# Moving a spectrum's halves across partitions by transfers on the SyncE queue instead of ScalarE copies, one item ahead

## The chip, the core and the metric

The kernel runs on one core of a Trainium2 chip. The core's engines are TensorE (matmuls, PE in the profile, with its weight loads as PEld), VectorE (DVE), ScalarE (ACT), GpSimd (POOL) and SyncE (SP), which here only issues transfers. Each engine works through its own instructions in a fixed order, written when the program is built, and waits at the head of that order for semaphores. SBUF has 128 partitions; matmul results land in the banks of PSUM. The metric is the device time of one execution in microseconds (us), the median of several runs.

## What is computed

The reference runs four layers in turn on a sequence of 2048 positions with 576 channels: a Fourier mixing layer, a gated long convolution, and both again.

```python
x = x + A(layernorm(x))      # real part of a 2-D DFT: Cr @ (n @ Wr) - Ci @ (n @ Wi)
x = x + B(layernorm(x))      # q * (irfft(rfft(kv) * rfft(ssm_k)) + kv * ssm_D), q = layernorm(x)
x = x + A(layernorm(x))
x = x + B(layernorm(x))
```

Here `kv` is a short convolution of `k` times `v`, the same in both B layers and independent of `x`. So the long convolution of `kv` with `ssm_k` has to be done once, and it can run beside the first A layer.

## The kernel before

**The main work.** In the first A layer (`layer`) TensorE multiplies the normalized rows with the sequence DFT matrix `c_mat`. A c-step (`tb`, `g`, `k`) loads one 128x512 block of it on SP's queue, splits it into a rounded high part (ScalarE, L91) and a remainder (VectorE, L92), and does 12 products of 512 columns into the four banks `s` and two into the bank `rm`. After 16 steps the banks are evacuated as `u`. After two groups of 16 the hidden-dimension products of the block before (`hidden`, L267, 27 products of 288 columns a piece) come in pieces between the c-steps. There are 4 blocks, and each gives 8 pieces; 24 of the pieces lie in the stretch of the change, three blocks' worth.

**The branch beside it.** The convolution is a generator, `branch` (L338), whose pieces are issued between the c-steps. It is a long DFT done as 128 points by 16 by 128 points. Its first stage writes its results to DRAM (`t_d`). The **16-point stage** reads them back as 64 items: for each of two halves `hf` of the channels, 32 groups `qg` of frequencies. An item has 128 partitions, and its columns hold the signal (288) and the kernel `ssm_k` (288). After the 16-point DFT, partitions 0 to 63 (`lo`) hold the real parts of a spectrum and 64 to 127 (`hi`) the imaginary ones. The last stage (`i2_products`) follows, in part between the last items.

For each item the stage does this:

- `load_feed` loads the item on SP's queue (tile `land`, two buffers), and `split_feed` splits it into rounded part (ScalarE) and remainder (VectorE, L492). Both run two items or more ahead.
- `mid_kernel` multiplies the kernel's columns with the 16-point DFT (three products of 288 columns into a bank of PSUM) and brings the spectrum into SBUF as `kk`, in four ScalarE instructions. `kk` has two halves of 288 columns and two buffers. The complex product needs the imaginary part beside the real one, in the partitions of the other, so three of the four copy 64 partitions from one half of the partitions to the other.
- `mid_signal` does the same DFT for the signal, and then four VectorE instructions, L505 to L508, make the complex product: `p1` overwrites `kk[:, 0, :]`, `p2` is a tile of its own.
- `mid_round` splits the product of the item before (ScalarE, then VectorE at L492), and `mid_inverse` does the inverse 16-point DFT of an item two further back, evacuates it (ScalarE) and stores it from ScalarE's queue.

The three banks `bk` serve all of these and the pieces of `hidden`.

**What sets the order.** `act` (L483) chains all ScalarE instructions of this stage in the order in which they are written. Loads with `load_after` stay behind the last `c_mat` load issued on SP's queue. Everything else is placed by a scheduler that simulates the engines at build time and issues on each engine what is ready, by the order in which it was written. The numbers that `branch` yields are shares of a budget: the main loop resumes it as its own steps pass, 3.1 for an item (0.4 + 1.6 + 1.1) and `I2_COST` = 2.0 for a piece of the last stage, 64 x 3.1 + 32 x 2.0 in all.

Of the kernel before, what the change touches and what calls it, by code (L numbers as in the profile page):

```python
# [12 lines left out]
AF = mybir.ActivationFunctionType  # L13
OP = mybir.AluOpType
# [7 lines left out]
HD = D // 2  # L22
# [22 lines left out]
I2_COST = 2.0  # L45
# [19 lines left out]
def fnet_h3_kernel(ctx: ExitStack, tc: tile.TileContext, x, c_mat, w_re, w_im, k_pad, v, shift_k,  # L65
                   ssm_k, ssm_d, f1c, i2c, midc, out):
    nc = tc.nc
# [56 lines left out]
    def lay(t, at, *sizes):  # L124

        for name, words, n in sizes:
            ring.setdefault(name, Ring()).tiles.extend(t[:, at + i * words:at + (i + 1) * words] for i in range(n))
            at += n * words
        assert at <= t.shape[1], (at, t.shape, sizes)
        return at  # L130

    def fresh(*names):
        for name in names:
            ring[name] = Ring()

    def two(v):
        return v.rearrange("p (a n) -> p a n", a=2)
# [200 lines left out]
    def branch():  # L338
# [133 lines left out]
        lo, hi = slice(0, 64), slice(64, 128)  # L472

        def mid_half(df, o):
            ps = bank()
            mm(ps[:, :HD], mc[:, 0, :], df[0][:, o:o + HD], True, False)
            mm(ps[:, :HD], mc[:, 0, :], df[1][:, o:o + HD], False, False)
            mm(ps[:, :HD], mc[:, 1, :], df[0][:, o:o + HD], False, True)
            return ps
# [3 lines left out]
        def act(*args, **kw):  # L483
            if last_act:
                with tc.issue_after(last_act[-1]):
                    last_act.append(nc.scalar.activation(*args, **kw).ins)  # L486
            else:
                last_act.append(nc.scalar.activation(*args, **kw).ins)
# [4 lines left out]

        def mid_kernel(df):
            pk, kk = mid_half(df, HD), two(ring["kk"]())
            act(kk[:, 0, :], pk[:, :HD], AF.Copy)
            act(kk[lo, 1, :], kk[hi, 0, :], AF.Copy)
            act(kk[hi, 1, :], kk[hi, 0, :], AF.Copy, scale=-1.0)
            act(kk[hi, 0, :], kk[lo, 0, :], AF.Copy)
            return kk  # L500

        def mid_signal(df, kk):
            px = mid_half(df, 0)
            p1, p2 = kk[:, 0, :], ring["p2"]()
            nc.vector.tensor_tensor(p1, px[:, :HD], p1, OP.mult)  # L505
            nc.vector.tensor_tensor(p2[lo], px[hi, :HD], kk[hi, 1, :], OP.mult)
            nc.vector.tensor_tensor(p2[hi], px[lo, :HD], kk[lo, 1, :], OP.mult)
            nc.vector.tensor_tensor(p1, p1, p2, OP.add)  # L508
            return p1

        def mid_round(p1):
            yf = two(ring["yf"]())
            act_split(yf[:, 0, :], yf[:, 1, :], p1)
            return yf

        def mid_inverse(hf, qg, yf):
            pv = bank()
            mm(pv[:, :HD], mc[:, 2, :], yf[:, 0, :], True, False)
            mm(pv[:, :HD], mc[:, 2, :], yf[:, 1, :], False, False)
            mm(pv[:, :HD], mc[:, 3, :], yf[:, 0, :], False, True)  # L520
            vo = ring["vo"]()
            act(vo, pv[:, :HD], AF.Copy)
            nc.scalar.dma_start(v_d[hf][4 * qg:4 * qg + 4].rearrange("q j c d -> (q j c) d"), vo)

        def i2_products(hf, j, fc, vf):
            yo = ring["vo"]()
            ps = bank()
            for c in range(2):
                cs = slice(c * HD, (c + 1) * HD)
                mm(ps[:, :HD], fc[:, c, :], vf[0][:, cs], c == 0, False)  # L530
                mm(ps[:, :HD], fc[:, c, :], vf[1][:, cs], False, False)
                mm(ps[:, :HD], fc[:, 2 + c, :], vf[0][:, cs], False, c == 1)
            act(yo, ps[:, :HD], AF.Copy)
            nc.scalar.dma_start(yb_d[j][:, hf * HD:(hf + 1) * HD], yo)
# [3 lines left out]
        feeds = []  # L538
# [7 lines left out]
        landed, halves, fcs, yfs = {}, {}, {}, []  # L546

        def load_feed(i):
            if i < len(feeds):
                kind, hf, q = feeds[i]  # L550
                landed[i] = ring["land"]()
                load_after(landed[i], v_d[hf][:, q].rearrange("p c d -> p (c d)") if kind else
                           t_d[hf][4 * q:4 * q + 4].rearrange("q j c s d -> (q j c) (s d)"))

        def load_fc(k):
            if k < len(rows):
                fcs[k] = quads(ring["fc"]())
                load_fr(fcs[k], i2c[rows[k]])

        def split_feed(i):  # L560
            if i < len(feeds):
                halves[i] = parts("df")
                act_split(*halves[i], landed.pop(i))
# [4 lines left out]
        for i in range(2):  # L568
            split_feed(i)
            load_feed(i + 2)  # L570
            load_fc(i)
        used, ahead, product = 0, 2, None
        for i, (kind, hf, q) in enumerate(feeds):
            df = halves.pop(i)
            if kind:
                i2_products(hf, q, fcs.pop(used), df)
                load_fc(used + ahead)
                used += 1
            else:
                if len(yfs) == MID_LAG:  # L580
                    mid_inverse(*yfs.pop(0))
                    yield 0.4
                kk = mid_kernel(df)
                if product is not None:
                    yfs.append((*product[:2], mid_round(product[2])))
                yield 1.6
                product = hf, q, mid_signal(df, kk)
            split_feed(i + 2)
            load_feed(i + ahead + 2)
            if i == last_mid:  # L590
                yield 0.4
                mid_inverse(*yfs.pop(0))
                yfs.append((*product[:2], mid_round(product[2])))
                while yfs:
                    yield 0.4
                    mid_inverse(*yfs.pop(0))
                for name, t, at, words in (("fc", m1, spare, 4 * P), ("land", flts, kk_at, D)):
                    old = ring[name]
                    held = [old.tiles[(old.n + m) % 2] for m in range(2)]
                    fresh(name)  # L600
                    lay(t, at, (name, words, 2))
                    ring[name].tiles.extend(held)
                for m in range(2):
                    load_fc(used + ahead + m)
                    load_feed(i + ahead + 3 + m)
                ahead = 4
            yield I2_COST if kind else 1.1

    def sums(src, junk):
        m = ring["stat"]()  # L610
# [96 lines left out]
    pending = []  # L707
    lay(flts, SC_AT, ("craw", NT, CRAW))
    br = branch()
    wl = load_w()  # L710
    load_x(0)
# [10 lines left out]
    used = 4  # L722
# [382 lines left out]
```

## Time and profile before

| | |
|---|---|
| median of 3 runs | 1205.37 us (1202.85 to 1206.05) |
| the profiled execution's span | 1202.1 us; its own time is not given apart from the three runs, whose fastest is 0.7 above the span |
| PE busy | 1181.4 us, 98% |
| VectorE busy | 840.0 us, 70% |
| ScalarE busy | 666.5 us, 55% |
| transfers | 261.95 MB, 218 GB/s over the span |
| 16-point stage | from about 214 to 550 us; the rest of the branch to about 616 |

The granted clock of TensorE has a mean of 0.997. How to read the rows: a group has its line, engine, operation, the tile written and the tiles read, the shape, and a count; then busy us and the mean ns of one instruction, then the idle time before them and what ended it. In a row in order of time, start and duration come first, and a bracket tells how long the engine was idle and who released it. The tile `flts` holds many small buffers, `kk`, `land`, `p2` and the raw `c_mat` blocks among them; `mid` holds the split items, `mats` the main operands. Since the ScalarE instructions of the stage come out of one helper, they all carry line L486, and are told apart by tile and shape: `flts<-bk` is an evacuation, `flts<-flts 64x288` a copy between partitions, `mid<-flts 128x288` the rounding of a product, `mid<-flts 128x576` the split of an item. A matmul's duration includes its way through the array; the distance between two starts is what it occupies.

### The profile page before, as it was taken

What the parts mean: (1) busy time and instruction counts of PE and PEld (TensorE: products, weight loads), DVE (VectorE), ACT (ScalarE), POOL (GpSimd) and SP (SyncE); (2) the same over time, 40 slices, a digit from 0 to 9 for tenths busy, and PEclk for the clock granted to TensorE, in tenths of its full rate; (3) what the DMA queues carried; (4) which work ended last, traced back from release to release, by engine and by line L of the source; (5) the groups of instructions that cost most, each with busy time, mean ns of one, the idle gap of its engine ahead of it and who ended that gap; (6) DMA issues with size and microseconds to landing.
All of it is one profiled execution on the core that took longest, in us unless ns stands there. A gap on an engine that the chain in (4) does not pass through costs nothing.

```text
span 1202.1 us, 18251 instructions
## 1 busy us (share of the span) xinstructions
PE 1181.4 (98%) x6320; PEld 1026.7 (85%) x6320; DVE 840.0 (70%) x1498; ACT 666.5 (55%) x1335; POOL 74.1 (6%) x116
## 2 busy tenths in 40 slices
PE   7999999999999999999999999999999999999997
PEld 5888888988888888888988898888888888789997
DVE  7899983678777677675347766775776777774764
ACT  6965665669877768675435666544444445450210
POOL 2200000000000000001101121000000000001111
PEclk9999999999999999999999999999999999999999
DMA  9879898546656666648967686872682686794621
GB/s 337 288 235 306 289 295 260 180 139 178 216 178 200 211 180 202 189 147 244 307 204 237 221 257 211 272 266 72 215 283 71 205 286 220 265 352 143 219 95 40
DMA packets 146110, 261.95 MB, mean 218 GB/s; under 512 B 15841, under 2 KB 44769, under 8 KB 146018
## 3 DMA queue, kind: packets, MB, share of 16 engines
q1 hardware_dynamic: 102674, 205.58, 53.2%
q10 hardware_dynamic: 36432, 42.63, 10.2%
q0 software_dynamic: 6912, 12.59, 3.9%
q8 instruction: 49, 0.80, 0.3%
q14 instruction: 43, 0.35, 0.1%
HBM read 194.09 MB, written 66.65 MB: 217 GB/s over the span
## 4 chain that ended last, share of the span: by engine, by line
PE 89%; DMA 3%; DVE 3%; ACT 3%; issue 1%; SPq 0%; POOLq 0%; ACTq 0%; POOL 0%; DVEq 0%
PE s L74 51%; PE bk L74 33%; PE rm L74 5%; DMA flts<-in_c_mat 1%; ACT flts L486 1%; DMA t<-ud 1%; ACT mid L486 0%; DMA t<-flts 0%; DVE mid L492 0%; DMA flts<-vd 0%; DMA flts<-in_ssm_k 0%; ACT u L91 0%; ACT mats L91 0%; DVE flts L172 0%; DVE mats L92 0%
## 5 line engine op out<-in xcount | busy, mean ns | idle before, releaser
L74 PE MATMUL s<-mats 128*128 128x512 f32 x2088 | 530.4, 392 | 0.4 <-DVE u L92 0.2
L74 PEld LDWEIGHTS s<-mats 128*128 128x128 f32 x2088 | 381.3, 188 | 70.6 <-DVE u L92 0.9
L92 DVE TENSOR_TENSOR mats<-flts,mats 128x512 fp32r<-128x512 f32 x206 | 141.1, 688 | 60.0 <-ACT mats L91 56.8
L91 ACT ACTIVATE mats<-flts 128x512 fp32r<-128x512 f32 x206 | 128.7, 627 | 86.4 <-PE bk L74 31.9
L74 PE MATMUL bk<-mid 128*128 128x288 f32 x768 | 131.2, 300 | 2.5 <-ACT flts L486 1.5
L74 PEld LDWEIGHTS bk<-mid 128*128 128x128 f32 x768 | 114.3, 188 | 22.1 <-ACT flts L486 9.0
L492 DVE TENSOR_TENSOR mid<-flts,mid 128x576 fp32r<-128x576 f32 (+1 forms) x160 | 101.9, 637 | 33.8 <-ACT mid L486 29.5
L74 PE MATMUL bk<-w,u 128*128 128x288 f32 x864 | 120.8, 295 | 0.1
L74 PEld LDWEIGHTS bk<-w,u 128*128 128x128 f32 x864 | 117.3, 188 | 3.6 <-ACT flts L486 1.2
L486 ACT ACTIVATE flts<-bk 128x288 f32<-128x288 f32 x160 | 61.9, 404 | 86.2 <-PE bk L74 69.8
L74 PE MATMUL rm<-mats 128*128 128x512 f32 x304 | 94.8, 390 | 0.0
L486 ACT ACTIVATE mid<-flts 128x576 fp32r<-128x576 f32 (+1 forms) x159 | 87.0, 582 | 7.5 <-DMA flts<-t 3.0
L486 ACT ACTIVATE flts<-flts 64x288 f32<-64x288 f32 x192 | 85.0, 443 | 5.9 <-ACT flts L486 0.4
L432 ACT ACTIVATE flts<-bk 128x288 f32<-128x288 f32 x128 | 49.4, 409 | 46.6 <-PE bk L74 40.1
L74 PE MATMUL bk<-f1r 128*128 128x288 f32 x384 | 66.0, 305 | 8.7 <-ACT f1r L91 6.8
L74 PEld LDWEIGHTS bk<-f1r 128*128 128x128 f32 x384 | 60.3, 194 | 16.0 <-ACT f1r L91 7.3
L74 PE MATMUL bk<-mats 128*128 128x288 f32 (+1 forms) x376 | 67.8, 317 | 0.0
L74 PEld LDWEIGHTS rm<-mats 128*128 128x128 f32 x304 | 56.9, 188 | 12.0 <-DVE flts L264 0.3
L278 DVE TENSOR_TENSOR flts<-flts,bk 128x288 f32<-128x288 f32 x48 | 21.7, 453 | 63.2 <-PE bk L74 63.2
L74 PE MATMUL s<-t,mats 128*128 128x512 f32 x264 | 65.5, 389 | 0.4 <-DVE t L92 0.4
L175 POOL TENSOR_TENSOR flts<-flts 128x1 f32<-128x1 f32 x35 | 28.5, 816 | 524.9 <-DVE flts L174 524.9
L74 PE MATMUL bk<-mats,t 128*128 128x288 f32 (+1 forms) x368 | 59.3, 303 | 0.0
(143 smaller groups left out, 1490.3 us busy)
## 6 DMA issues: line engine op xcount, KB each, us to landing
flts<-in_c_mat SPq DMA_DIRECT2D x148, 256.0 KB, 3.6
ph<-in_c_mat SPq DMA_DIRECT2D x54, 512.0 KB, 4.2
t<-flts ACTq DMA_DIRECT2D x64, 288.0 KB, 4.6
flts<-t SPq DMA_DIRECT2D x64, 288.0 KB, 2.9
flts<-in_c_mat SPq DMA_DIRECT2D x30, 512.0 KB, 4.9
vd<-flts ACTq DMA_DIRECT2D x64, 144.0 KB, 2.3
flts<-vd SPq DMA_DIRECT2D x32, 288.0 KB, 4.8
mid<-in_i2c POOLq DMA_DIRECT2D x32, 256.0 KB, 5.1
```

The lines of the kernel that those rows point to most:

```text
L74: nc.tensor.matmul(ps, lhsT, rhs, start=first, stop=last, skip_group_check=more)
L91: a = nc.scalar.activation(h, src, AF.Copy).ins
L92: return a, nc.vector.tensor_tensor(l, src, h.bitcast(F32), OP.subtract).ins
L175: pows.append(nc.gpsimd.tensor_tensor(rs, ve, mhalf, OP.pow).ins)
L278: added[:] = [nc.vector.tensor_tensor(r[:, cs], r[:, cs], ps[:, :HD], OP.add).ins]
L432: stored[:] = [nc.scalar.activation(so[:, c, :], ps[:, :HD], AF.Copy).ins]
L486: last_act.append(nc.scalar.activation(*args, **kw).ins)
L492: nc.vector.tensor_tensor(l, src, h.bitcast(F32), OP.subtract)
```

## The change

The kernel's spectrum comes out of PSUM in two ScalarE instructions of 64 partitions each, one straight into the first half of `kk`, the other into the second. Two transfers on SP's queue, inside SBUF, fill the other two quarters. The sign that one copy used to put in now stands in the VectorE instruction that uses it. The kernel's products and these transfers are issued for item i+1 ahead of the signal's products of item i; where a piece of the last stage stands between two items, at its end. For the two buffers of `kk` to suffice, the rounding of item i-1's product now stands ahead of the kernel products of item i+1, where it stood behind those of item i.

```diff
         def mid_kernel(df):
             pk, kk = mid_half(df, HD), two(ring["kk"]())
-            act(kk[:, 0, :], pk[:, :HD], AF.Copy)
-            act(kk[lo, 1, :], kk[hi, 0, :], AF.Copy)
-            act(kk[hi, 1, :], kk[hi, 0, :], AF.Copy, scale=-1.0)
-            act(kk[hi, 0, :], kk[lo, 0, :], AF.Copy)
+            act(kk[lo, 0, :], pk[lo, :HD], AF.Copy)
+            act(kk[hi, 1, :], pk[hi, :HD], AF.Copy)
+            nc.sync.dma_start(kk[hi, 0, :], kk[lo, 0, :])
+            nc.sync.dma_start(kk[lo, 1, :], kk[hi, 1, :])
             return kk
...
-            nc.vector.tensor_tensor(p2[lo], px[hi, :HD], kk[hi, 1, :], OP.mult)
+            nc.vector.scalar_tensor_tensor(p2[lo], px[hi, :HD], -1.0, kk[hi, 1, :], op0=OP.mult, op1=OP.mult)
...
-        used, ahead, product = 0, 2, None
+        used, ahead, product, spectra = 0, 2, None, {}
+
+        def kernel_ahead(i):
+            if i < len(feeds) and not feeds[i][0]:
+                spectra[i] = mid_kernel(halves[i])
+                return True
+
+        kernel_ahead(0)
         for i, (kind, hf, q) in enumerate(feeds):
             df = halves.pop(i)
             if kind:
                 i2_products(hf, q, fcs.pop(used), df)
                 load_fc(used + ahead)
                 used += 1
+                if kernel_ahead(i + 1):
+                    yield 1.2
             else:
                 if len(yfs) == MID_LAG:
                     mid_inverse(*yfs.pop(0))
                     yield 0.4
-                kk = mid_kernel(df)
                 if product is not None:
                     yfs.append((*product[:2], mid_round(product[2])))
-                yield 1.6
-                product = hf, q, mid_signal(df, kk)
+                if kernel_ahead(i + 1):
+                    yield 1.2
+                product = hf, q, mid_signal(df, spectra.pop(i))
...
-            yield I2_COST if kind else 1.1
+            yield I2_COST if kind else 1.5
```

## The prediction

> **What bounds the kernel now.** I read the page first (busy shares), then the table of stretches, then the order of time inside the 16-point stage, and last the waits.
>
> ```profile
> span 1202.1 us, 18251 instructions
> PE 1181.4 (98%) x6320; PEld 1026.7 (85%) x6320; DVE 840.0 (70%) x1498; ACT 666.5 (55%) x1335; POOL 74.1 (6%) x116
> 300.00:340.00 40.00, 39.56 (x205) 33.79 (x204) 33.10 (x65) 34.27 (x71) 0.00 (x0) 1.00 0.64 202
> ```
>
> TensorE is busy all along. The third line is one stretch of the stage: PE 39.56 of 40 us, DVE 33.10, ACT 34.27, clock 1.00, DMA share 0.64. ScalarE is loaded, but it is not the engine without gaps. The stage's steady part, in order of time (start, duration, engine, line), shows it:
>
> ```profile
> 305.49 1.53 PE L74 MATMUL s<-mats 128*128 128x512 f32 x6
> ...
> 306.19 0.41 ACT L486 ACTIVATE flts<-bk 128x288 f32<-128x288 f32 x1 [0.49 <-DVE flts L508]
> 306.63 1.37 ACT L486 ACTIVATE flts<-flts 64x288 f32<-64x288 f32 x3
> ...
> 308.03 1.02 ACT L486 ACTIVATE mid<-flts 128x288 fp32r<-128x288 f32 x2
> 308.04 0.46 DVE L505 TENSOR_TENSOR flts<-bk,flts 128x288 f32<-128x288 f32 x1 [1.26 <-ACT flts L486]
> 308.51 0.46 DVE L492 TENSOR_TENSOR mid<-flts,mid 128x288 fp32r<-128x288 f32 x1
> ...
> 309.48 0.45 DVE L507 TENSOR_TENSOR flts<-bk,flts 64x288 f32<-64x288 f32 x1
> ...
> 309.88 1.53 PE L74 MATMUL s<-mats 128*128 128x512 f32 x6
> ...
> 310.64 0.45 DVE L508 TENSOR_TENSOR flts<-flts 128x288 f32<-128x288 f32 x1
> 310.75 0.32 SPq L159 DMA_DIRECT2D flts<-t  x1
> ...
> 311.72 0.33 SPq L159 DMA_DIRECT2D flts<-in_c_mat  x1
> ...
> 317.83 0.63 ACT L91 ACTIVATE mats<-flts 128x512 fp32r<-128x512 f32 x1
> ...
> 309.25 0.80 PE bk L74 x6
> 310.04 1.37 PE s L74 x6
> ```
>
> One c-step lasts 309.88 - 305.49 = 4.39 us and carries one item. The last two rows are from the chain that ended last: six 512-column products take 1.37 (0.228 each), six of 288 columns 0.80 (0.133 each). A step has 12 products of the `s` banks, two of the remainder and 9 of the item: 14 x 0.228 + 9 x 0.133 = 4.39. There is nothing to gain in a step of this kind, whatever ScalarE does. What can be gained are the places where TensorE waits for the item. All waits of 220 to 550 us that touch the change (total, times, longest), the last one SP's own:
>
> ```profile
> DVE flts L505 <- ACT flts L486: 36.5, 24, 2.7
> PEld bk L74 <- ACT flts L486: 10.1, 27, 1.0
> PEld bk L74 <- DVE flts L507: 3.0, 7, 0.9
> ACT mid L486 <- DMA flts<-t: 3.0, 5, 0.9
> SPq L159 <- DVE mid L492: 173.7, 73, 5.8
> ```
>
> The waits of the weight load are not all lost, since a load runs ahead of its matmul. One such place (the first four rows; the last two belong to the part on the transfers):
>
> ```profile
> 335.00 1.52 PE L74 MATMUL s<-mats 128*128 128x512 f32 x6
> ...
> 336.45 0.45 DVE L507 TENSOR_TENSOR flts<-bk,flts 64x288 f32<-64x288 f32 x1
> ...
> 336.95 0.43 PEld L74 LDWEIGHTS bk<-mid 128*128 128x128 f32 x3 [0.86 <-DVE flts L507]
> 336.95 0.66 PE L74 MATMUL bk<-mid 128*128 128x288 f32 x3 [0.44 <-DVE flts L507]
> ...
> 346.14 0.46 DVE L505 TENSOR_TENSOR flts<-bk,flts 128x288 f32<-128x288 f32 x1 [2.65 <-ACT flts L486]
> ...
> 353.15 0.46 DVE L505 TENSOR_TENSOR flts<-bk,flts 128x288 f32<-128x288 f32 x1
> ```
>
> Six products from 335.00 at 0.228 would have let the next begin at 336.37; it began at 336.95. So 0.58 of the 0.86 was lost and 0.28 was covered. Applied to all: 10.1 - 27 x 0.28 = 2.5 us lost behind ScalarE's evacuations, 3.0 - 7 x 0.28 = 1.0 behind the products' last read of their bank. Waits shorter than 0.28 lose nothing instead of a negative amount, so the true sum is somewhat above 3.5; I put 5 us as the ceiling of what this change can win.
>
> **The change part by part.** Durations by line, from 220 to 550 us (and one from 214 to 616):
>
> ```profile
> L486 ACT ACTIVATE flts<-flts 64x288 f32<-64x288 f32 x192 | 85.0, 443 | 5.9 <-ACT flts L486 0.4
> L486 ACT ACTIVATE flts<-bk 128x288 f32<-128x288 f32 x135 | 51.7, 404 | 54.8 <-PE bk L74 46.7 <-ACT flts L486 5.5 <-DVE flts L508 1.0
> L486 ACT ACTIVATE mid<-flts 128x288 fp32r<-128x288 f32 x62 | 27.6, 445 | 2.3 <-DVE flts L508 0.8
> L492 DVE TENSOR_TENSOR mid<-flts,mid 128x288 fp32r<-128x288 f32 x62 | 28.2, 456 | 11.1 <-ACT mid L486 10.7
> L506 DVE TENSOR_TENSOR flts<-bk,flts 64x288 f32<-64x288 f32 x63 | 29.0, 460 | 1.7
> L492 DVE TENSOR_TENSOR mid<-flts,mid 128x576 fp32r<-128x576 f32 x75 | 56.8, 758 | 3.7 <-ACT mid L486 1.7
> ...
> L232 DVE SCALAR_TENSOR_TENSOR w<-flts,w 128x576 fp32r<-128x576 f32 (+1 forms) x2 | 1.5, 757 | 0.1
> ```
>
> *Removed on ScalarE.* Per item one evacuation of 128x288 (404 ns) and three copies of 64x288 (443 each): 1.73 us. In their place two evacuations of 64x288. ScalarE's time goes by columns, not partitions (443 for 64x288, 445 for 128x288 out of the same tile), so each is 404: 0.81. Saved: 0.92 x 64 = 59 us of ScalarE. As PE has no gap in a steady step, what this is worth is 0 to 5 us (the ceiling). I take half, -2.5: the evacuations that came late behind three copies come earlier, but the second edit below puts something else in front of half of them.
>
> *The multiplication by -1 on VectorE.* L506 becomes a scalar_tensor_tensor. At 128x576 this form took 757 ns, the plain one 758: nothing. Bounds: 0 and a few hundredths per item, on an engine with a gap of 1.26 us ahead of L505.
>
> *The rounding of the last product goes ahead of the kernel's evacuation.* There are two `kk` buffers, and the products of item i+1 now go into the one whose product i-1 is being rounded. So in ScalarE's fixed order the first evacuation of item i+1 stands behind the rounding (445) and must wait for VectorE's subtraction, which reads the same buffer. By the rows at 308.03 and 308.51 that subtraction ended at 308.97, 0.94 after the rounding began. Before, this bank was released 0.41 after the inverse's; now 0.94 + 2 x 0.40 = 1.74: its bank is held 1.3 us longer, and behind ScalarE's wait stand the next split of a feed and whatever c split is queued there. For 64 items that is 86 us of a bank held longer. What reaches TensorE of such a delay is shown by the nearest row of the same three banks: VectorE waited 36.5 us for ScalarE with the signal's bank full, and TensorE lost 1.0 us behind it. By that share 86 us cost 2.4. Bounds: 0 (the freed 0.92 pays for it) and 13 x 0.94 = 12 (half of the 27 waits for ScalarE's evacuations are for this bank, and each grows in full). I take +2.3.
>
> *Two transfers on SP.* No transfer inside SBUF stands in this trace. Nearest are these, with us to landing:
>
> ```profile
> flts<-t SPq DMA_DIRECT2D x62, 288.0 KB, 2.9
> flts<-in_c_mat SPq DMA_DIRECT2D x53, 256.0 KB, 3.1
> vd<-flts ACTq DMA_DIRECT2D x61, 144.0 KB, 2.3
> DMA to landing us min/median/max: 2.6/2.9/6.1
> ```
>
> (the last line is for the `t` loads). The new ones hold 64 x 288 x 4 bytes, 72 KB, each, and they are issued right beside a `t` and a `c_mat` load, as the rows at 310.75 and 311.72 show. Lower bound 2.3 (the store of 144 KB), upper 6.1; I take 2.9, the loads on the same queue, plus 0.32 for the second's issue: 3.2. Is it hidden? The buffer goes round once in two items: four products of VectorE 4 x 0.455 = 1.82 and a feed's subtraction among them 0.76, rounding and subtraction 0.94, two evacuations 0.81, issue 0.32: 4.65 us, and then the transfer; with 3.2 it is 7.85. Two steady items last 8.78, so up to 4.1 us of landing are hidden. After a hidden-layer piece items come closer: from the L505 at 346.14 to the one at 353.15, two items later, are 7.0 us. Of the 62 such distances between the stage's 64 L505, 13 are shorter than 7.85, by 9 us together. That is VectorE's lateness at most; by the share above (1.0 of 36.5) 0.3 of it reach TensorE. Bounds: 0 and the 9 in full; I take +0.3. If the cover is gone, each us of landing over 4.1 costs a us per two items, 32 us in all.
>
> The Trainium skill, page "DMA: Bandwidth & Descriptors", section "Anatomy of one DMA — SWDGE (gpsimd) path", gives about 2.0 us plus bytes / 436e3 for one DMA: an estimate of 2.2 by that page, with which both transfers would be hidden everywhere and this term 0. That fit is for the other kind of queue; the rows above are slower.
>
> *SP's queue.* Two issues more per item, 0.64 us, beside 0.65 for the two loads now; SP idles for most of a step, 173.7 us of it waiting to reload a feed. A transfer's wait for ScalarE's evacuation holds up the next c load and feed load behind it. A feed's split comes after that evacuation in ScalarE's order, so its reload is ready later anyway: 0. A c load issued at 311.72 lands 3.1 later, at 314.8, and is split at 317.83 (two buffers; the split between takes the other): 3 us of slack, so 0. Where feeds are late already (3.0 us in five places) it may be a few tenths; bounds 0 and 1.5, inside the rounding of the sum.
>
> *Order of issue.* Per item the pacing still adds up to 3.1 (0.4 + 1.6 + 1.1 before, 0.4 + 1.2 + 1.5 now); only the first kernel product comes without a share, 1.2 of the stage's 262 (64 x 3.1 + 32 x 2.0): nothing. The first item waits once for a transfer (0 to 2.9 us); TensorE has c-steps to do: 0.
>
> Sum: -2.5 + 2.3 + 0.3 = +0.1 us. Against the profiled execution: 1202.1 of span to 1202.2. The median of the runs, 1205.37, lies 3.3 above that span, and I leave that as it is: 1205.5.
>
> **The rivals.**
>
> *Faster: ScalarE's relief counts in full.* For it: the copies lead directly to the longest waits of VectorE (2.65 at 346.14). The bank of the signal is emptied as soon as it is full, and the rounding finds VectorE idle. Then all of the ceiling goes: 1205.4 - 5 = 1200.4. Against it: ScalarE's new wait inside the same order.
>
> *Slower: the evacuation behind the rounding becomes TensorE's wait.* There are three banks, and a piece of the hidden layer holds one for its 27 products; with the kernel's held 1.3 us longer, one is left. Half of the 27 waits, each 0.94 longer, is +12, less the 2.5 won: 1205.4 + 9.5 = 1215 at worst, and with half of them 1209.5. I price it at 1211. It decides as soon as more than six of these waits grow in full. Against it: in a steady step the item has 4.39 us and the bank is needed again a whole item later.
>
> *Slower: the transfers land late.* If the second half waits for the first and both for the load ahead of them, landing grows from 3.2 to half as much again, 4.8; that is 0.7 over the 4.1 that two steady items hide, x 32 pairs = 22, and if only the pairs beside a late load are hit, half of it: 1205.4 + 11 = 1216. It decides from a landing of 4.1 us. For it: `t` loads reached 6.1. Against it: their median is 2.9. A rule of the Trainium skill, page "DMA: Bandwidth & Descriptors", section "Rules for kernel authors", speaks for this one: two transfers to disjoint partition halves serialize, and one should use a single transfer of 128 partitions. No transfer in this trace shows that.
>
> **How the numbers follow.** What a measurement of this kernel can tell from no change is about 0.3%, 3.6 us. No change (1205.5, from 1201.8 to 1209): 0.36. Faster in full: 0.28. Rounding ahead of the evacuation: 0.21. Late transfers: 0.15. So faster 0.28, same 0.36, slower 0.36. The range goes from 1200 (the full ceiling) to 1213.5, leaving out 0.06 below and 0.13 above; the likeliest case's own range is 1201.8 to 1209.
>
> **What would show it.** Right, if VectorE's L505 no longer waits for ScalarE, the steady step is still 4.39 us, the new transfers land in 2.3 to 3.5 us, and ScalarE's first half evacuation waits for the subtraction of the rounding, 0.3 to 0.9 us per item. TensorE's weight loads for the item should still wait some 10 to 14 us. The faster rival shows as that sum falling below 6; the second rival as it passing 20, with ScalarE's half evacuations named as the releaser; the third as VectorE's products waiting for a transfer for over 20 us in total. The prediction is wrong if the items' order on TensorE changes so much that stalls at the borders of the c blocks or at the stage's two ends grow to several us each.

## The result: slower by 0.75%

The changed kernel took 1214.17 us (1213.29 to 1214.56, 4 runs) against 1204.85 us for the kernel before, in the same comparison. The ratio is 1.0075, with a 95% interval of 1.0061 to 1.0089: 9 us. The forecast was no change, 1205.5 us, with a range up to 1213.5. The time lies just outside the range, and the likeliest case did not come.

The profiled execution has a span of 1212.6 us. The page of the changed kernel, its busy row and the one stretch shown before:

```profile
span 1212.6 us, 18555 instructions
PE 1186.9 (98%) x6320; PEld 1027.3 (85%) x6320; DVE 840.7 (69%) x1498; ACT 615.9 (51%) x1207; POOL 74.0 (6%) x116
...
300.00:340.00 40.00, 40.00 (x204) 33.88 (x203) 31.66 (x63) 26.16 (x54) 0.00 (x0) 1.00 0.77 231
```

ScalarE fell from 666.5 to 615.9 us, 51 of the 59 us that the sum said. TensorE's busy time rose by 5.5 us for the same 6320 matmuls and its share stayed at 98%; so busy shares tell nothing here, and the waits do. The waits of 220 to 560 us in the changed kernel (total, times, longest), the last two SP's own:

```profile
ACT flts L486 <- DVE mid L492: 23.4, 32, 3.8
...
ACT mid L486 <- DVE flts L508: 14.8, 18, 1.8
PEld bk L74 <- ACT mid L486: 10.5, 20, 1.1
...
PEld bk L74 <- DVE mid L492: 8.7, 18, 1.3
DVE flts L505 <- DMA flts<-flts: 6.0, 6, 2.9
...
PEld bk L74 <- ACT flts L486: 3.9, 11, 0.6
...
PEld bk L74 <- DVE flts L507: 0.2, 1, 0.2
...
SPq L498 <- ACT flts L486: 91.4, 56, 4.3
SPq L159 <- DVE mid L492: 70.6, 65, 4.0
```

The waits that the change was to remove did fall: TensorE behind ScalarE's evacuations from 10.1 to 3.9 us, behind L507 from 3.0 to 0.2. VectorE's wait for the kernel's spectrum went from 36.5 (for ScalarE) to 6.0 us (for transfers). In their place stands a wait that the kernel before hardly had (0.7 us): TensorE's weight loads for the item wait 10.5 + 8.7 us for the tile `mid`, that is, for the split of a feed, first its rounded part (ScalarE), then its remainder (VectorE). And ScalarE waits 23.4 us with its evacuations for the rounding's subtraction, in 32 of the 64 items, most often 0.58 to 0.59 us.

How the one wait leads to the other shows best among the hidden-layer pieces at the start of the stage. In order of time:

```profile
228.86 0.44 ACT L486 ACTIVATE mid<-flts 128x288 fp32r<-128x288 f32 x1 [2.42 <-issue]
229.34 0.46 DVE L492 TENSOR_TENSOR mid<-flts,mid 128x288 fp32r<-128x288 f32 x1 [0.56 <-ACT mid L486]
229.89 0.84 ACT L486 ACTIVATE flts<-bk 64x288 f32<-64x288 f32 x2 [0.58 <-DVE mid L492]
...
230.75 0.68 ACT L486 ACTIVATE mid<-flts 128x576 fp32r<-128x576 f32 x1
...
231.48 0.19 PEld L74 LDWEIGHTS bk<-mid 128*128 128x128 f32 x1 [1.09 <-ACT mid L486]
```

The last product is rounded, its subtraction follows on VectorE, only then come the two half evacuations of the kernel's spectrum (0.58 us of waiting in front of them), and behind them the split of the feed two items on. The kernel's products of that very feed are what TensorE wants next, and their first load waits 1.09 us for the split.

In the stretch without hidden-layer pieces four steps in a row became longer, from about 318 to 336 us:

```profile
319.14 0.41 ACT L486 ACTIVATE flts<-bk 128x288 f32<-128x288 f32 x1
...
319.48 0.45 ACT L486 ACTIVATE mid<-flts 128x288 fp32r<-128x288 f32 x1
319.50 1.54 PE L74 MATMUL s<-mats 128*128 128x512 f32 x6
...
319.97 0.45 DVE L492 TENSOR_TENSOR mid<-flts,mid 128x288 fp32r<-128x288 f32 x1
...
320.52 0.84 ACT L486 ACTIVATE flts<-bk 64x288 f32<-64x288 f32 x2 [0.59 <-DVE mid L492]
...
321.38 0.69 ACT L486 ACTIVATE mid<-flts 128x576 fp32r<-128x576 f32 x1
321.47 0.46 DVE L505 TENSOR_TENSOR flts<-bk,flts 128x288 f32<-128x288 f32 x1 [1.05 <-PE bk L74]
...
322.43 0.45 DVE L507 TENSOR_TENSOR flts<-bk,flts 64x288 f32<-64x288 f32 x1
...
322.92 0.76 DVE L492 TENSOR_TENSOR mid<-flts,mid 128x576 fp32r<-128x576 f32 x1
...
323.10 1.16 PE L74 MATMUL bk<-mid 128*128 128x288 f32 x6
...
323.73 0.30 PEld L74 LDWEIGHTS bk<-mid 128*128 128x128 f32 x2 [0.18 <-DVE mid L492]
...
324.10 1.54 PE L74 MATMUL s<-mats 128*128 128x512 f32 x6
```

From 319.50 to 324.10 are 4.60 us, where TensorE's own work is 4.39. The same chain runs here with the same 0.59 us of waiting, but it is not what comes last: the split's rounded part is done at 322.07, and its remainder begins at 322.92, behind L505 to L507 in VectorE's order, which had waited 1.05 us for the signal's products on TensorE. The kernel's products then wait 0.18 us for that remainder. So this step is a loop from the signal's products over VectorE to the kernel's products of the next step. It costs 0.2 us in each of the four steps, and the other steps of this stretch take about 4.4 us or less.

To compare kernels I add up, from the trace, the distances between successive starts of matmuls beyond the usual ones (0.132 us for 288 columns, 0.227 for 512), where they exceed 15 ns, between 214 and 570 us of the span: 12.6 us before, 22.4 us after. The difference of 9.8 us is the slowdown (the spans differ by 10.5, the medians by 9.3). Both traces hold 6320 matmuls, so missing records do not make the difference. By stretch, 214 to 292 us went from 4.1 to 8.2, 292 to 338 stayed at 0.8, and 338 to 570 went from 7.7 to 13.4; the kernels run shifted by some us, so these borders are rough. The stretch of the long steps thus adds nothing to the difference; the loss lies ahead of it and behind it, where other pieces stand between the items. Where the trace names what released the weight load or the matmul behind such a distance, 11.1 of the 22.4 us end with the split of a feed (5.7 its rounded part, 5.4 its remainder), and 0.3 of the 12.6 in the kernel before.

### The profile page after: what moved, and what is told of

It is laid out like the page before. It is cut to its first block, busy times and chain, and to the rows that moved or that the text cites. A ratio compares the mean times of both kernels' runs of the same rounds, so it can differ in the third digit from the quotient of the medians.

```text
span 1212.6 us, 18555 instructions
## 1 busy us (share of the span) xinstructions
PE 1186.9 (98%) x6320; PEld 1027.3 (85%) x6320; DVE 840.7 (69%) x1498; ACT 615.9 (51%) x1207; POOL 74.0 (6%) x116
## 4 chain that ended last, share of the span: by engine, by line
PE 82%; DMA 6%; DVE 5%; ACT 3%; issue 3%; SPq 0%; POOLq 0%; ACTq 0%; DVEq 0%
PE s L74 47%; PE bk L74 31%; PE rm L74 5%; DVE mid L492 2%; DMA t<-flts 1%; ACT mid L486 1%; DMA flts<-flts 1%; DMA early<-in_x 1%; ACT flts L486 1%; DMA flts<-t 1%; DVE flts L506 1%; DVE flts L507 1%; DMA t<-ud 1%; DMA mid<-in_i2c 0%; DMA flts<-in_c_mat 0%
## 5 line engine op out<-in xcount | busy, mean ns | idle before, releaser
L486 ACT ACTIVATE flts<-bk 64x288 f32<-64x288 f32 (+1 forms) x224 | 91.2, 408 | 121.7 <-PE bk L74 92.0
L74 PE MATMUL bk<-mid 128*128 128x288 f32 x768 | 137.4, 303 | 7.4 <-ACT mid L486 2.8
L486 ACT ACTIVATE mid<-flts 128x576 fp32r<-128x576 f32 (+1 forms) x159 | 92.2, 585 | 28.6 <-DVE flts L508 14.8
L432 ACT ACTIVATE flts<-bk 128x288 f32<-128x288 f32 x128 | 49.4, 409 | 46.6 <-PE bk L74 40.6
L74 PEld LDWEIGHTS s<-t,mats 128*128 128x128 f32 x264 | 49.5, 188 | 10.7 <-DVE t L92 0.5
```

The lines of the kernel that those rows point to most:

```text
L74: nc.tensor.matmul(ps, lhsT, rhs, start=first, stop=last, skip_group_check=more)
L432: stored[:] = [nc.scalar.activation(so[:, c, :], ps[:, :HD], AF.Copy).ins]
```

## The experiments

Two theories were left after the traces. **Lead**: the kernel's products now stand one item ahead, and with them the need for the feed's split; `split_feed` kept its place, so its lead shrank from two items to one. **Round**: the rounding now holds the `kk` buffer that the next evacuation wants, so ScalarE waits for VectorE in the middle of its fixed order. The rival was **transfers**: they land late or hold up SP's queue. All ratios are to the kernel before, in the same comparison, and the last column is the sum just defined (in e_short the stage runs on to about 614 us, so its sum falls short). The order on every engine is set anew when a kernel is built, so each edit also moves instructions that it does not name.

| run | what differs | us | ratio (95%) | lost by TensorE, us |
|---|---|---|---|---|
| after | the change | 1214.17 | 1.0075 (1.0061 to 1.0089) | 22.4 |
| e_copies | after, copies for transfers | 1220.79 | 1.0135 (1.0114 to 1.0156) | 29.9 |
| e_transfers | before, transfers for copies | 1221.44 | 1.0132 (1.0109 to 1.0154) | 28.6 |
| e_short | before, split one item later | 1255.81 | 1.0427 (1.0404 to 1.0451) | 55.3 |
| e_lead | after, split one item earlier | 1209.61 | 1.0040 (1.0026 to 1.0053) | 17.1 |
| e_late | control for e_lead | 1215.18 | 1.0084 (1.0070 to 1.0099) | 23.5 |
| e_sum | after, sum in another tile | 1209.18 | 1.0032 (1.0019 to 1.0044) | 17.0 |
| e_p2lead | e_sum and e_lead | 1206.80 | 1.0013 (0.9996 to 1.0029) | 15.4 |
| e_first | e_sum, evacuation ahead of rounding | 1217.83 | 1.0108 (1.0089 to 1.0127) | 25.7 |
| e_first_lead | e_first and e_lead | 1211.89 | 1.0064 (1.0046 to 1.0083) | 19.3 |
| e_poolq | after, transfers on GpSimd's queue | 1218.04 | 1.0108 (1.0092 to 1.0124) | 26.4 |
| e_p2leadpool | e_p2lead, GpSimd's queue | 1209.33 | 1.0031 (1.0019 to 1.0043) | 16.7 |

### One part of the change alone

e_copies keeps the new order and takes the transfers out:

```diff
-            act(kk[lo, 0, :], pk[lo, :HD], AF.Copy)
-            act(kk[hi, 1, :], pk[hi, :HD], AF.Copy)
-            nc.sync.dma_start(kk[hi, 0, :], kk[lo, 0, :])
-            nc.sync.dma_start(kk[lo, 1, :], kk[hi, 1, :])
+            (the four ScalarE instructions of before)
```

> The changed kernel's order of issue (kernel spectrum one item ahead, rounding in front of it) with the four ScalarE instructions of before in place of two evacuations and two transfers. If the SP transfers cost the 9 us (theory transfers): back to 1205 to 1207. If the feed's split is needed an item earlier (theory lead) or the evacuation waits behind the rounding (theory round): 1214 or more, since ScalarE carries 59 us more in the same order, and TensorE's weight loads for the item still wait 20 us and more for ScalarE and VectorE.

It took 1220.79 us, 0.6% more than the changed kernel, as theories lead and round had it. This run trades the transfers for the copies and so shows only that the trade is a gain in this order: with three copies more in front of it the split comes later, and TensorE waits 17.7 us for its rounded part instead of 10.5. That the transfers themselves cost the changed kernel little rests on VectorE's 6.0 us of waiting for them, and on e_p2lead below, which keeps them. The waits of 220 to 560 us:

```profile
PEld bk L74 <- ACT mid L486: 17.7, 25, 2.7
...
PEld bk L74 <- DVE mid L492: 8.7, 21, 1.0
```

e_transfers is the other half: `mid_kernel` and the sign as in the change, everything else as before.

> The order of before, with the two half evacuations and two SP transfers in place of the copies, so the transfers stand between the kernel's products and the signal's products of the same item. Theory transfers: 1214 or more, VectorE waiting 2 us and more per item for them. Theories lead and round: near before, 1203 to 1208, although VectorE now waits for transfers in most items, because a late product alone hardly reaches TensorE.

It took 1221.44 us, where theories lead and round expected 1203 to 1208 and theory transfers 1214 or more. In this order the transfers do cost: without the item's lead they lie open between the kernel's products and the signal's. That does not carry over to the changed kernel, where VectorE waits 6.0 us for them and not 27.9. In e_transfers it waits and holds the signal's bank:

```profile
DVE flts L505 <- DMA flts<-flts: 27.9, 23, 3.0
PEld bk L74 <- DVE flts L507: 18.3, 19, 2.1
...
PE bk L74 <- DVE flts L507: 10.9, 14, 1.6
```

With 28 us of waiting in front of L505, TensorE's loads wait 18.3 us behind L507. In the kernel before they waited 3.0 us with 36.5 us in front of L505. So the share of VectorE's lateness that reaches TensorE is no constant of this kernel, and it was the share on which two terms of the forecast rested, the rounding and the transfers. The transfers need the lead of an item, and each half of the change alone is worse than both together.

### The lead

e_short takes the kernel before and shortens the lead alone:

```diff
-        for i in range(2):
+        for i in range(1):
             split_feed(i)
             load_feed(i + 2)
...
-            split_feed(i + 2)
-            load_feed(i + ahead + 2)
+            split_feed(i + 1)
+            load_feed(i + ahead + 1)
```

> The kernel before, with one thing changed: each feed is loaded and split one item later, so that its 16-point products have the lead that the changed kernel's kernel products have. Theory lead: slower by 4 to 10 us, 1209 to 1214, and TensorE's item loads wait 10 us and more for the mid tile, which they hardly do now (about 1 us). If only the order of ScalarE's work is at fault (theory round): within 2 us of before.

It lost 52 us, five times what was expected, with the mark that was expected: the loads for the item wait 37.4 us for the split's rounded part, 55 times. Three rows of its order of time, one item apart:

```profile
301.35 0.19 PEld L74 LDWEIGHTS bk<-mid 128*128 128x128 f32 x1 [0.59 <-ACT mid L486]
...
306.57 0.19 PEld L74 LDWEIGHTS bk<-mid 128*128 128x128 f32 x1 [0.60 <-ACT mid L486]
...
311.79 0.19 PEld L74 LDWEIGHTS bk<-mid 128*128 128x128 f32 x1 [0.59 <-ACT mid L486]
```

From one item to the next are 5.22 us here instead of 4.39. That the loss is so much larger than the changed kernel's may be due to the three copies, which still stand in ScalarE's order here; this was not tested apart.

e_lead does the opposite to the changed kernel: `split_feed(i + 3)` and `load_feed(i + ahead + 3)`, three splits ahead of the loop, and `I2_FIRST` 38 for 37, because the last stage's first load would otherwise come before its data are stored.

> The changed kernel, with each feed loaded and split one item further ahead (and the last stage's pieces beginning one item later, because their loads would come too early otherwise), which gives the kernel's products the lead that they had before. Theory lead: 1204 to 1208, the item's weight loads no longer wait for the mid tile. Theory round: 1211 to 1215, waits move to ScalarE's evacuations. Theory transfers: 1214.

1209.61 us, between the two theories, with the marks of both: 0.35% of the 0.75% went. Its waits of 220 to 560 us:

```profile
ACT flts L486 <- DVE mid L492: 25.4, 34, 3.6
ACT mid L486 <- DVE flts L508: 23.3, 21, 2.8
PEld bk L74 <- ACT flts L486: 13.3, 27, 1.6
...
PEld bk L74 <- ACT mid L486: 1.3, 3, 0.5
```

TensorE's waits for the split are gone (10.5 to 1.3 us), and its waits for the evacuations are back (3.9 to 13.3), while ScalarE still waits 25.4 us for the subtraction. By the sum of lost distances, 5.4 us now end with the kernel's half evacuations, 0.6 in the changed kernel: with the split out of the way, the bank that the rounding's wait holds is a good part of what TensorE still waits for. The four longer steps are gone, as they are in e_sum:

```profile
315.62 1.53 PE L74 MATMUL s<-mats 128*128 128x512 f32 x6
...
320.01 1.53 PE L74 MATMUL s<-mats 128*128 128x512 f32 x6
...
324.40 1.53 PE L74 MATMUL s<-mats 128*128 128x512 f32 x6
```

e_late has the change of `I2_FIRST` alone.

> A control for the run with the longer lead: the changed kernel with only the last stage's pieces beginning one item later. If the longer lead itself gave back the 5 us: 1213 to 1215, as the changed kernel. If the later pieces did it: 1208 to 1211.

1215.18 us, as the changed kernel: the lead did it, not the later pieces.

### The rounding

e_sum frees the `kk` buffer earlier. The sum of the two products goes to `p2`, so the rounding reads that tile:

```diff
-        lay(flts, at, ("land", D, 2), ("kk", D, 2), ("vo", HD, 3), ("p2", HD, 1))
+        lay(flts, at, ("land", D, 2), ("kk", D, 2), ("p2", HD, 1), ("vo", HD, 3))
...
-            nc.vector.tensor_tensor(p1, p1, p2, OP.add)
-            return p1
+            nc.vector.tensor_tensor(p2, p1, p2, OP.add)
+            return p2
```

> The changed kernel with the sum of the products in the other product's tile, laid one place earlier so that no other buffer shares its words: the rounding no longer holds the kk buffer. In the run of this idea made before (with the tile where it was) about half of the loss went. Theory round as one of two causes: 1208 to 1211 again, ScalarE's evacuations waiting under 2 us for the subtraction of the rounding (23 us in the changed kernel).

An earlier form of it, e_p2, left `p2` where it was. There its last words are shared with a buffer of the block borders, so that at a border an item's product is overwritten; no work is left out. It took 1209.10 us, ratio 1.0042 (1.0025 to 1.0058).

> The changed kernel, but the sum of the two products is written to the other product's tile, so the kk buffer is free after the last of the four products and ScalarE's half evacuation no longer waits for the rounding's subtraction. Theory round: 1204 to 1208, TensorE's waits for the split feeds fall with it, since the split stands behind the evacuation in ScalarE's order. Theory lead: 1212 to 1215, ScalarE's wait for VectorE gone but TensorE's waits for the feeds stay. Theory transfers: 1214.

e_sum took 1209.18 us: again about half of the loss went. Its waits:

```profile
ACT mid L486 <- DVE flts L508: 32.0, 31, 2.5
PEld bk L74 <- DVE mid L492: 9.4, 22, 1.4
...
PEld bk L74 <- ACT mid L486: 6.0, 11, 1.4
...
PEld bk L74 <- ACT flts L486: 1.8, 5, 0.5
```

ScalarE's evacuations no longer wait for the subtraction (23.4 us before; no such row of any size is left), and TensorE's waits for the split's rounded part fall from 10.5 to 6.0. Those for the remainder stay (9.4).

e_p2lead has both edits.

> The changed kernel with both repairs: the sum of the products in the other product's tile (which is laid one place earlier, so that no other buffer shares its words), and the feeds split one item further ahead. Each alone gave back about 5 of the 9 us. If they are two separate costs: 1204 to 1206. If they are the same cost, seen twice: 1209 as with either.

1206.80 us, ratio 1.0013 (0.9996 to 1.0029): both repairs together gave back 0.62%, and what is left cannot be told from nothing. The single repairs gave 0.35% and 0.43%, so by the times the two costs nearly add up. By the lost distances they overlap: the repairs alone took away 5.3 and 5.4 us of the 22.4, both together 7.0. And the interval of e_p2lead overlaps those of the single ones. So it is not shown that they are two separate costs. The order of time above says why they need not be: the rounding's wait and the short lead are two links of one chain, from the rounding over the evacuations and the split to the kernel's products, and it can be cut at either. The lost distances by stretch, in us:

| stretch of the span | before | after | e_sum | e_lead | e_p2lead |
|---|---|---|---|---|---|
| 214 to 292 us | 4.1 | 8.2 | 6.6 | 8.6 | 8.2 |
| 292 to 338 us | 0.8 | 0.8 | 0.7 | 0.0 | 0.4 |
| 338 to 570 us | 7.7 | 13.4 | 9.7 | 8.4 | 6.8 |

With both repairs the later part of the stage loses less than before, and its start loses twice as much. What the start's loss consists of was not followed up. The waits of e_p2lead show where the expected gain went:

```profile
PEld bk L74 <- ACT flts L486: 7.4, 13, 1.7
...
PEld bk L74 <- DVE flts L507: 5.3, 8, 1.7
...
DVE flts L505 <- DMA flts<-flts: 2.7, 5, 0.9
```

TensorE waits 12.7 us for the item's banks, as against 13.1 in the kernel before. With some 50 us of work off ScalarE, and VectorE's 36.5 us of waiting gone, the banks come free no earlier in the few places where TensorE waits for them.

### The order on ScalarE, and the queue

e_first is e_sum with the kernel's products and evacuations issued ahead of the rounding again:

```diff
+                more = kernel_ahead(i + 1)
                 if product is not None:
                     yfs.append((*product[:2], mid_round(product[2])))
-                if kernel_ahead(i + 1):
+                if more:
                     yield 1.2
```

> The changed kernel with the sum of the products in the other product's tile, laid one place earlier, and the kernel's products and evacuations of the next item now issued ahead of the rounding, as before. Then the rounding no longer stands waiting for the sum in front of them on ScalarE. Theory round: the waits of ScalarE's rounding for the sum fall from 30 us to under 15, and the time to 1205 to 1208. Theory lead alone: 1209 to 1213, TensorE's waits for the mid tile stay over 10 us.

> The same as the run before it in this call (sum in the other product's tile, kernel's evacuations ahead of the rounding), with the feeds split one item further ahead as well. If lead and round are the two causes, what is left is ScalarE's relief: 1201 to 1205, TensorE's item loads waiting 10 us or less in all. If something else of the change costs (transfers, SP's queue, the order of TensorE's work): 1207 and more.

They took 1217.83 and 1211.89 us, each slower than its partner with the rounding in front (1209.18 and 1206.80). The first lies outside both ranges, the second in that for something else of the change that costs; as e_p2lead, which differs only in this order, is back within noise of before, it is this order that costs. ScalarE's waits for the sum did fall (from 32.0 to 9.1 us in e_first), but its evacuations wait more for TensorE:

```profile
ACT flts L486 <- PE bk L74: 91.2, 68, 3.6
PEld bk L74 <- ACT mid L486: 10.8, 23, 0.8
```

In e_sum that wait is 63.4 us. The evacuation now stands at the head of ScalarE's order before its products are done, with the rounding and the split behind it. That this is the whole cause was not tested; in e_first_lead, where the split is no longer urgent, the loss is 0.5% against e_p2lead all the same. So, with the buffer of its own, the rounding's new place is the better one; what it cost in the changed kernel came with the buffer that it shared.

e_poolq and e_p2leadpool issue the two transfers on GpSimd's queue, nothing else.

> The changed kernel with its two transfers issued from GpSimd's queue instead of SP's. If SP's queue, held up by a transfer's wait for ScalarE, costs through late feeds and c blocks: 1207 to 1211, and ScalarE's waits for feeds fall. If the landing of the transfers is what costs, they come later from that queue: 1216 or more. Theories lead and round: 1213 to 1217.

> Both repairs (sum in the other product's tile, feeds split one item further ahead) with the transfers on GpSimd's queue. With both repairs and SP's queue the time was that of before within 0.3%. If SP's queue is the last cost left: 1200 to 1203, faster than before. If not: 1205 to 1209.

Neither is faster than with SP's queue: e_poolq is 0.33% slower, and the 0.18% of e_p2leadpool lie within the two intervals. SP stood 91.4 us waiting with a transfer at its head, and freeing it of that gained nothing. The 1218.04 us of e_poolq lie where late landing was expected, but VectorE's wait for transfers at L505 is 4.8 us there against 6.0, so its trace does not bear that out. In e_p2leadpool it is 13.0 us instead of 2.7. Why GpSimd's queue is worse was not settled.

## Why the prediction was wrong

**Removed on ScalarE (-2.5, ceiling 5).** The durations held: a half evacuation is 406 ns (404 was said), the multiplication by -1 at L506 459 (460 before). The waits behind evacuations fell as the upper end said. But the term was taken for a gain in itself, and with the two costs repaired nothing of it could be measured (1.0013, 0.9996 to 1.0029).

**The rounding ahead of the evacuation (+2.3, bounds 0 and 12).** The wait was foreseen, its size for TensorE was not. ScalarE's wait is there in 32 of the 64 items, mostly 0.59 us (0.3 to 0.9 in each was said). Repairing it gave back 0.43%, 5 us, twice the term. The failing step is the share: "By that share 86 us cost 2.4" took 1.0 us lost of 36.5 us of VectorE's waiting and carried it over to a wait of another engine. ScalarE's wait does not only hold a bank, which is how it was priced. It delays all that stands behind it in ScalarE's order, the split above all: of the lost distances 11.1 us end with the split of a feed and 0.6 with a half evacuation.

**The split of the feed: the term that was missing.** The prediction noted that behind ScalarE's wait "stand the next split of a feed", and in the part on SP that the split comes after the evacuation, and concluded "its reload is ready later anyway: 0". It asked when the split's input is ready, and not who waits for its output. The change moved the reader of the split, the kernel's products, one item ahead and left the split in its place. Repairing the lead gave back 0.35%, 4 us, some of it the same us as the repair of the rounding. So a term was put at nothing that should have been several us. The sentence "There is nothing to gain in a step of this kind" was right, and little was lost in those steps either (four of 4.60 us); more was lost with hidden-layer pieces between the items, and for a late split there the sum had nothing.

**Two transfers on SP (+0.3).** About right. Landing was 2.8 us for the first and 2.4 for the second (3.2 was taken with the issue), VectorE waited 6.0 us for them in all, and e_copies shows that the trade for the copies is worth more than it costs. The cover named for them, an item of lead, is what e_transfers took away: +1.3%.

```profile
flts<-t SPq DMA_DIRECT2D x62, 288.0 KB, 3.2
...
flts<-flts SPq DMA_DIRECT2D x128, 72.0 KB, 2.6
...
DMA to landing us min/median/max: 1.9/2.8/5.2
...
DMA to landing us min/median/max: 2.0/2.4/4.8
```

(The issues of the changed kernel between 220 and 560 us, then the landing of L498's and of L499's transfers.) The 2.2 us that was worked out from the fit of the Trainium skill, page "DMA: Bandwidth & Descriptors", section "Anatomy of one DMA — SWDGE (gpsimd) path", is 0.4 below the median of both, 2.6, and the 2.9 that was taken is 0.3 above it. (Nor were all the rows of before slower than that fit: the store of 144 KB took 2.3, and the fit gives an estimate of 2.3 for it.) And 2.2 would not have hidden them everywhere by the prediction's own distances: with the second issue the round is then 4.65 + 2.2 + 0.32 = 7.17 us, and 8 of the 62 distances are shorter. The rule of the Trainium skill, same page, section "Rules for kernel authors", that two transfers to disjoint partition halves serialize, spoke for the third rival. By the trace the second was issued 0.56 us after the first and landed 0.26 us after it (medians of 64 and of 50 pairs, as far as both landings are on record), so the two were under way together; whether their data moved one after the other within that time the trace does not show.

**SP's queue (0).** Right as far as the runs go: another queue gained nothing. The two issues take 1.0 us per item (0.64 was said). The sentence that leads to this 0 is the one quoted above, and it is where the split was passed over.

**The rivals.** The second one (+6, rounding) named a right place and price (5 us by the repair) and the wrong way to TensorE: its mark was ScalarE's half evacuations as the releaser, for over 20 us. The sum of the item's load waits did pass 20 (10.5 + 8.7 + 3.9 = 23.1), with the split as the releaser. (With half of +12, less 2.5, its sum gives 1208.9 and not 1209.5.) The third (late transfers) did not come about: VectorE waited 6.0 us for transfers, not 20. One sign of being wrong that the prediction named, stalls that grow to several us at an end of the stage, came near: the start, 214 to 292 us, lost 4.1 us more, in several places.

## What to carry to other kernels

When a piece of work is moved ahead, move everything that feeds it, or count how much lead its inputs lose: here a load's split that had two items of lead was left with one, and its place at the end of another engine's fixed order, behind a new wait, became what TensorE waited for. The losses lay where the work is irregular; a look at the steady part alone would have missed them. When an edit puts an instruction ahead of another because they share a buffer, look for the wait this puts into the middle of an in-order engine, and price it by what stands behind it, not by the bank that it holds. A share of one wait that reached the bottleneck, read off a trace, holds for that wait alone.

## What the runs showed of the hardware that was not expected

Issuing a transfer inside SBUF kept SP's queue 0.47 us for the first and 0.55 for the second (medians; up to 1.4), where the loads of 256 and 288 KB take 0.32 to 0.33. And 128 of them, 9.4 MB of a total that was 262, went with a later landing of the feeds' loads beside them, 3.2 instead of 2.9 us (medians); that the transfers are the cause was not tested.
